# Attention with one shared key and value head, plus a gated MLP: a fifth of the exps on VectorE, all engine orders from one planner, layer norm streamed into the first group

## The chip, the cores and the metric

One core of one Trainium2 chip. The metric is the device time in microseconds (us) of one execution, the median of several runs; lower is better. Besides the time, each run gives the span of the core in the profile and the mean TensorE clock that was granted in it, as a share of full speed.

Engine names as in the profile: PE is the TensorE matmul, PEld its weight load, DVE is VectorE, ACT is ScalarE, POOL is GpSimd, SP is the DMA-issuing SyncEngine.

## The reference

```python
B, S, D, H, F = 1, 2048, 512, 32, 1792        # head size 16, all bf16
def reference(A_x, A_wq, A_wk, A_wv, A_wo, B_x, B_w1, B_w2):
    xn = layernorm(A_x)                        # eps 1e-5
    q = (xn @ A_wq) -> [1, 32, 2048, 16]       # 32 query heads
    k = xn @ A_wk ; v = xn @ A_wv              # one key and one value head, 16 wide
    p = softmax(q k^T * 16**-0.5)
    s = concat_heads(p v) @ A_wo
    g = silu(silu(xn @ B_w1) @ B_w2)
    return A_x + s * g
```

The softmax has 32 x 2048 x 2048 = 134 million exps. Held with keys on partitions, that is 1.05 million columns of 128, or 2048 *score tiles* of 128 keys x 512 queries. This sets the scale of everything below.

## The kernel before

The scores are taken in units of four and of two tiles, alternately, each unit in its own set of PSUM banks. ScalarE turns a unit into bf16 probabilities with one exp, and PE multiplies them with the values. Everything else (projections, MLP, output) is cut into small *jobs* between the units. A column of ones next to the values gives the softmax denominator. PSUM is the memory that PE writes its results into, used here as eight banks of 512 columns. Below, the score matmuls of one unit are a *score phase*; when they write into banks that ScalarE has just read, they are a *refill*; and matmuls with the values that go side by side into one bank are a *value round*. The silu of the MLP is computed by way of a tanh on ScalarE.

```python
NFILL = 1; NFILL_START = 3; NFILL_TAIL = 2          # dummy matmuls per unit
...
# units of 4 and 2 score tiles: banks 0..3 and 4..5
n = 4 if par == 0 else 2
...
# PE: the scores of a unit, then matmuls with a zero tile (they add nothing)
def emit_S(u, nfill=0):
    if u >= 2:
        pe.wait_ge(act_sem.sem, u - 1)              # ScalarE has read this set of banks
    for k, (c, g, kt, i) in enumerate(units[u]):    # four row tiles of 32 partitions
        h = pe.matmul(bank(b0 + k), lhsT=kT_sb[32*i:32*i+KP, kt*P:(kt+1)*P],
                      rhs=qT_sb[32*i:32*i+KP, c % 2, g, :], ..., tile_position=(32*i, 0))
        if last:
            for fi in range(nfill):
                h = pe.matmul(bank(b0 + k), lhsT=zero_sb[:, :], rhs=xnT_sb[:, 0, 0:NQ],
                              start=False, stop=(fi == nfill - 1))
    h.then_inc(s_sem.sem, 1)
...
# ScalarE
a.activation(p_sb[:, u % NPB, 0:n*NQ], ps[:, b0*512:(b0+n)*512], ACT.Exp)
...
# layer norm in two halves of 1024 rows: bn_stats on VectorE, Sqrt on ScalarE
# (a second activation table), transposes, K, V, Q; the first exp comes after both halves
```

The softmax here doesn't subtract the row's maximum and nothing guards it: scores larger than these inputs give would overflow.

## Time and profile before

1020.22 us, median of 3 runs (1019.31 to 1020.82).

The first lines are the page's busy times and shares of the span, then the granted clock in 40 slices (in tenths of full speed).

```profile
span 1014.8 us, 12867 instructions
...
PE 811.4 (80%) x5406; PEld 220.8 (22%) x5406; DVE 197.7 (19%) x346; ACT 977.1 (96%) x786; POOL 10.4 (1%) x13
...
PEclk8999999999999999999999999999999999999998
```

ScalarE is busy 96% of the time and VectorE 19%.

The groups of instructions, shapes kept apart (busy us, mean ns of one, idle time before them and what ended it):

```profile
L565 ACT ACTIVATE p_sb<-ps 128x2048 bf16<-128x2048 f32 x341 | 686.9, 2014 | 9.0 <-PE ps L674 3.5 <-PE ps L668 0.5
L565 ACT ACTIVATE p_sb<-ps 128x1024 bf16<-128x1024 f32 x342 | 398.9, 1166 | 1.2 <-PE ps L668 0.6 <-PE ps L674 0.5
L674 PE MATMUL ps<-xnT_sb,zero_sb 128*128 128x512 bf16 x458 | 158.8, 387 | 0.0
```

The two exp groups add up to more than ScalarE's busy time, because one ACTIVATE starts before the recorded end of the one before it. "Busy" and "idle" therefore hide small gaps. What an exp really costs is read from the distance between the start times of neighbours. Its smallest value is 1.756 us after a 2048-column exp, 0.903 after a 1024-column one and 0.476 after a 512-column tanh. From 512 to 1024 to 2048 columns it grows by 0.427 us for each 512, so I estimate from these three that a column costs 0.833 ns and a start about 50 ns. What a step takes beyond that minimum I call a **gap**. All gaps below are computed in this way from the start times of exps and tanhs.

The timeline of ScalarE at the start (start, length, both in us):

```profile
0.73 1.28 ACT L498 ACT_TABLE_LOAD   x1 [0.73 <-PEq L819]
...
20.41 0.20 ACT L498 ACTIVATE rstd_sb<-rstd_sb 128x8 f32<-128x8 f32 x1
...
24.03 1.28 ACT L522 ACT_TABLE_LOAD   x1
...
35.18 1.88 ACT L565 ACTIVATE p_sb<-ps 128x2048 bf16<-128x2048 f32 x1 [0.48 <-PE ps L674]
```

With these readings the span before is: 35.2 us until the first exp, 942.3 us of ScalarE work (341 x 1.757 + 342 x 0.903 + 72 x 0.477), 26.4 us of gaps, and 10.8 us after the last exp. Together 1014.7 of 1014.8.

### The profile page before, as it was taken

The numbers are of one execution on the slowest core, as the hardware profiler recorded it, in microseconds if no ns is written. First come the engines' busy times: TensorE is split into PE (matmuls) and PEld (weight loads), VectorE is DVE, ScalarE is ACT, GpSimd is POOL, SyncE is SP. The second block draws the span as 40 slices with busy tenths as digits, with TensorE's granted clock in tenths as the row PEclk, the third lists the DMA queues.
The fourth block names the chain that finished last, engine by engine and source line by source line (L and its number), as shares of the span: only waits on it lengthen the run. The fifth ranks groups of instructions, "written<-read, shape, count | busy, mean of one in ns | idle before, by whom it ended". The sixth has DMA issues, their size and how long they took to land.

```text
span 1014.8 us, 12867 instructions
## 1 busy us (share of the span) xinstructions
PE 811.4 (80%) x5406; PEld 220.8 (22%) x5406; DVE 197.7 (19%) x346; ACT 977.1 (96%) x786; POOL 10.4 (1%) x13
## 2 busy tenths in 40 slices
PE   3887778877788888777888887778878888888885
PEld 2322222222222222222222222222222222222221
DVE  6122122222111222212112211222102111100113
ACT  5799999999999999999999999999999999999995
POOL 4000000000000000000000000000000000000000
PEclk8999999999999999999999999999999999999998
DMA  9000000000000000000000000000000000000000
GB/s 270 1 1 1 1 1 1 1 1 1 1 1 1 12 11 1 1 1 1 1 1 11 11 1 1 1 1 2 1 1 11 11 1 1 1 1 1 2 1 21
DMA packets 7369, 9.76 MB, mean 10 GB/s; under 512 B 1488, under 2 KB 6608, under 8 KB 7312
## 3 DMA queue, kind: packets, MB, share of 16 engines
q1 hardware_dynamic: 6576, 5.28, 1.9%
q0 software_dynamic: 736, 3.67, 1.0%
q8 instruction: 42, 0.69, 0.3%
q14 instruction: 15, 0.12, 0.0%
HBM read 6.85 MB, written 2.10 MB: 9 GB/s over the span
## 4 chain that ended last, share of the span: by engine, by line
ACT 49%; PE 32%; issue 15%; DVE 3%; DMA 0%; ACTq 0%; DVEq 0%
ACT p_sb L565 45%; PE ps L668 11%; PE ps L696 9%; PE ps L674 6%; ACT t_sb L555 3%; PE ps L736 2%; PE ps L729 1%; PE ps L742 1%; DVE oraw_sb L399 1%; PE ps L771 1%; PE ps L762 1%; PE ps L594 1%; DVE stats_sb L359 0%; DMA x_sb<-in_A_x_dram 0%; ACT xnT_sb L521 0%
## 5 line engine op out<-in xcount | busy, mean ns | idle before, releaser
L565 ACT ACTIVATE p_sb<-ps 128x1024 bf16<-128x1024 f32 (+1 forms) x683 | 949.4, 1590 | 10.2 <-PE ps L674 4.0
L668 PE MATMUL ps<-qT_sb,kT_sb 32*128 32x512 bf16 x2048 | 267.5, 385 | 164.5 <-ACT p_sb L565 163.2
L696 PE MATMUL ps<-p_sb,vaug_sb 128*32 128x512 bf16 x2048 | 274.4, 390 | 9.2 <-DVE oraw_sb L399 8.5
L674 PE MATMUL ps<-xnT_sb,zero_sb 128*128 128x512 bf16 x458 | 158.8, 387 | 0.0
L668 PEld LDWEIGHTS ps<-qT_sb,kT_sb 32*128 32x128 bf16 x2048 | 66.7, 91 | 412.9 <-ACT p_sb L565 390.6
L696 PEld LDWEIGHTS ps<-p_sb,vaug_sb 128*32 128x32 bf16 x2048 | 68.9, 93 | 187.7 <-issue 152.0
L434 DVE SCALAR_TENSOR_TENSOR u_sb<-t_sb,ps 128x512 bf16<-128x512 bf16 x56 | 38.5, 687 | 263.7 <-ACT t_sb L555 263.7
L736 PE MATMUL ps<-w_sb,u_sb 128*128 128x512 bf16 x224 | 67.8, 385 | 0.7 <-DVE tmp_sb L438 0.7
L729 PE MATMUL ps<-xnT_sb,w_sb 128*128 128x512 bf16 x224 | 67.8, 385 | 0.0
L399 DVE CAST oraw_sb<-ps 128x512 bf16<-128x512 f32 x32 | 22.1, 692 | 203.8 <-PE ps L696 203.8
L555 ACT ACTIVATE t_sb<-ps 128x512 bf16<-128x512 f32 x72 | 60.0, 833 | 0.0
L674 PEld LDWEIGHTS ps<-xnT_sb,zero_sb 128*128 128x128 bf16 x458 | 35.4, 96 | 78.7 <-issue 78.0
L445 DVE TENSOR_SCALAR qT_sb<-ps 128x512 bf16<-128x512 f32 x30 | 20.6, 685 | 109.1 <-PE ps L742 109.1
L438 DVE SCALAR_TENSOR_TENSOR tmp_sb<-t_sb,ps 128x512 bf16<-128x512 bf16 x16 | 11.0, 686 | 138.5 <-ACT t_sb L555 138.5
L742 PE MATMUL ps<-xnT_sb,wqp_sb 128*128 128x512 bf16 x120 | 36.3, 385 | 0.0
L771 PE MATMUL ps<-wop_sb,xn_sb 128*128 128x512 bf16 x96 | 29.1, 385 | 0.0
L401 DVE STREAM_TRANSPOSE otr_sb<-oraw_sb 128x512 bf16<-128x512 bf16 x32 | 22.8, 712 | 1.1
L414 DVE STREAM_TRANSPOSE xn_sb<-otr_sb 128x512 bf16<-128x512 bf16 x32 | 22.8, 711 | 1.1
L418 DVE SCALAR_TENSOR_TENSOR fin_sb<-ps,tmp_sb 128x512 bf16<-128x512 f32 x12 | 8.3, 692 | 63.7 <-PE ps L771 63.7
L736 PEld LDWEIGHTS ps<-w_sb,u_sb 128*128 128x128 bf16 x224 | 12.7, 97 | 26.2 <-issue 25.2
L729 PEld LDWEIGHTS ps<-xnT_sb,w_sb 128*128 128x128 bf16 x224 | 12.8, 97 | 25.4 <-issue 25.4
L582 PE MATMUL ps<-ident,xn_sb 128*128 128x128 bf16 x64 | 5.1, 256 | 12.4 <-DVE xn_sb L376 12.4
(53 smaller groups left out, 125.8 us busy)
## 6 DMA issues: line engine op xcount, KB each, us to landing
w_sb<-in_B_w_dram POOLq DMA_DIRECT2D x2, 1792.0 KB, 13.1
x_sb<-in_A_x_dram SPq DMA_DIRECT2D x4, 512.0 KB, 5.8
out_dram<-ob_sb SPq DMA_DIRECT2D x16, 128.0 KB, 1.7
wqn_sb<-in_A_wq_dram SPq DMA_DIRECT2D x1, 512.0 KB, 7.9
wop_sb<-in_A_wo_dram SPq DMA_DIRECT2D x4, 128.0 KB, 6.6
wkn_sb<-in_A_wk_dram SPq DMA_DIRECT2D x1, 16.0 KB, 6.9
wv_sb<-in_A_wv_dram SPq DMA_DIRECT2D x1, 16.0 KB, 6.7
```

Of the source, the lines that this page charges most:

```text
L399: v.tensor_copy(oraw_sb[:, sl, :], bank(OB)).then_inc(o_sem.sem, 1)
L401: v.transpose(otr_sb[:, sl, :], oraw_sb[:, sl, :]).then_inc(dv.sem, 1)
L434: v.scalar_tensor_tensor(out=u_sb[:, tc % 2, ft, :], in0=t_sb[:, ti % 2, :], scalar=1.0, in1=bank(FB), op0=ALU.add, op1=ALU.mult).then_inc ...
L555: a.activation(t_sb[:, ti % 2, :], bank(FB), ACT.Tanh, scale=scale).then_inc(t_sem.sem, 1)
L565: a.activation(p_sb[:, u % NPB, 0:n * NQ], ps[:, b0 * 512:(b0 + n) * 512], ACT.Exp).then_inc(act_sem.sem, 1)
L668: h = pe.matmul(bank(b0 + k), lhsT=kT_sb[32 * i:32 * i + KP, kt * P:(kt + 1) * P], rhs=qT_sb[32 * i:32 * i + KP, c % 2, g, :], start=True, ...
L674: h = pe.matmul(bank(b0 + k), lhsT=zero_sb[:, :], rhs=xnT_sb[:, 0, 0:NQ], start=False, stop=(fi == nfill - 1))
L696: h = pe.matmul(bank(OB)[32 * i:32 * (i + 1), :], lhsT=vaug_sb[:, kt, :], rhs=p_sb[:, u % NPB, k * NQ:(k + 1) * NQ], start=(kt == 0), stop ...
L729: h = pe.matmul(bank(FB), lhsT=w1_sb[:, dc, ft * P:(ft + 1) * P], rhs=xnT_sb[:, dc, tc * NQ:(tc + 1) * NQ], start=(dc == 0), stop=(dc == N ...
L736: h = pe.matmul(bank(FB), lhsT=u_sb[:, tc % 2, ft, (tt % 4) * P:(tt % 4 + 1) * P], rhs=w2_sb[:, ft, :], start=(ft == 0), stop=(ft == NFT - 1))
L742: h = pe.matmul(bank(FB), lhsT=wqp_sb[:, dc, g, :], rhs=xnT_sb[:, dc, c * NQ:(c + 1) * NQ], start=(dc == 0), stop=(dc == NDC - 1))
L771: h = pe.matmul(bank(FB), lhsT=on_sb[:, (c % 2) * NG + g, (tt % 4) * P:(tt % 4 + 1) * P], rhs=wop_sb[:, g, :], start=(g == 0), stop=(g == ...
```

## The change

The intent is to take exps off the busiest engine and give them to an idle one, VectorE, without using an exp there. For a bf16 number, adding a constant to the 16-bit pattern of 2^y moves y. So VectorE computes `round(128*log2(e)*x + const)` as a 16-bit integer from the scores (the *conversion*); read as bf16 this is e^x with a straight line between powers of two. Five more integers, made by adding 21, 43, 64, 85 and 107 (the *shifts*), give the same line at other places within the octave. A weighted sum of the six is close to e^x. The weights are put into six copies of the value tile, so PE forms the sum while it multiplies with the values, at the price of six value matmuls per tile instead of one.

At the same time the whole kernel is rewritten. Every operation is a task with an estimated duration; one planner walks all engines through time and fixes each engine's order and semaphores at build time. Units become three and two tiles. The projections run as four column tiles of 32, the same array mode as the value matmuls. The dummy matmuls go. Layer norm runs in four chunks of 512 rows with `pow` on GpSimd instead of `Sqrt` on ScalarE, and the first group of heads starts when the first chunk is ready.

```diff
-NFILL = 1
-NFILL_START = 3
-NFILL_TAIL = 2
+SHIFT = (0, 21, 43, 64, 85, 107)
+SHIFT_W = (0.23925781, 0.21875, 0.19824219, 0.16210938, 0.15820312, 0.13769531)
+SHIFT_BETA = -0.603400124
+MM = 216.0
+SWITCH = 105.0
+DVE_LIMIT = 2500.0
+S_TOL = 30.0
...
+class Planner:            # clk, order and tasks per engine; place(), finalize(), run_engine()
...
+    A_BANKS = ((0, 1, 2), (3, 4))          # units of three and two tiles
...
+        for j in range(K + 1):             # K = 6
+            pl.add(Task(DV, 260.0, lambda v, j=j: v.memset(v_sb[:, j, :, :], 1.0 if j == 0 else SHIFT_W[j - 1]),
+                        (), [("V", j, c) for c in range(NC)], 0))
...
+            t2 = pl.add(Task(PO, 400.0, lambda g, a=a, b=b: g.tensor_tensor(
+                rstd_sb[:, a:b], rstd_sb[:, a:b], half_sb[:, 0:4], ALU.pow), ...
...
+                    bt.P[i] = pl.add(Task(DV, 620.0, lambda v, b=b, i=i, bb=bt.b: v.tensor_scalar(
+                        db_sb[:, bb, i * NQ:(i + 1) * NQ], bank(b), 128.0 * LOG2E, 128.0 * SHIFT_BETA + 16256.0,
+                        op0=ALU.mult, op1=ALU.add), ...                     # the conversion, 16-bit integer out
...
+                    pl.add(Task(DV, 600.0, lambda v, s=s, j=j, bb=bt.b: v.tensor_scalar(
+                        ds_sb[:, s, :], db_sb[:, bb, :], SHIFT[j], None, op0=ALU.add), ...   # a shift, 4 tiles at once
...
+        def do_S(t): ...                   # scores of a unit, and of 0 to 2 tiles for VectorE
+        def do_pv(t, got): ...             # a value round: up to four column tiles into one bank
...
+            if ts is not None:             # a score refill is coming up: hold PE back for it
+                if ts <= t + 30: ...
+                elif col is not None:
+                    if max(ts, end) > max(ts, act_need() - 446.0) + S_TOL:
+                        pl.clk[PE] = ts
+                        return True
```

The emitted program has 334 exps of 1536 columns, 333 of 1024, 72 tanh, 380 conversions, 475 shifts and 3948 value matmuls.

## The prediction

> **What bounds the kernel now.** ScalarE. The page's busy table has ACT at 977.1 of 1014.8 us (96%), PE 811 (80%, with 158.8 us of dummy matmuls against a zero tile), DVE 197.7 (19%). From the start times of neighbouring ACTIVATEs in the trace, a 2048-column exp holds ScalarE 1.756 us at least, a 1024-column one 0.903, a tanh 0.476: 0.833 ns per column plus 50 ns each. 341 x 1.756 + 342 x 0.903 + 72 x 0.476 = 942 us. The first exp starts at 35.2 us, the last work of ScalarE ends at 1004, then an 11 us tail. So 967 us of exp phase hold 942 of work and about 25 of hand-over gaps: the 1024-column exp is followed after 0.913 us at the median but 1.13 at the 95th percentile, because PE refills four banks late.
>
> **What changes.**
> 1. 380 of 2048 score tiles (19%) leave ScalarE, counted in the emitted program. It keeps 334 exps of 1536 columns (1.33 us) and 333 of 1024 (0.903), plus 72 tanh: 444 + 301 + 34 = 779 us, a saving of 163.
> 2. VectorE gains 380 affine conversions from PSUM (0.62 us spacing) = 236 us, and 475 shifts over 2048 16-bit columns in SBUF. The trace has none. [...] With old duties (tanh products 44, norm 49, prologue 25, rest 26) about 665 us.
> 3. PE drops the dummies; each moved tile needs six value matmuls instead of one. 3948 value matmuls in 1179 rounds of up to four column tiles, 667 score phases, 592 projection rounds, at 216 ns each, plus 1314 tiling switches at about 100 ns (neighbouring starts of 310 to 321 instead of 216 ns): about 660 us.
> 4. Prologue: streaming the norm by four tiles, pow on GpSimd instead of Sqrt plus a second table load. First exp near 17 us instead of 35; some starvation follows while VectorE (6 us per chunk of keys) feeds a ScalarE that needs 7 us per chunk.
>
> **How much is on the path.** All ScalarE time was, so nearly all 163 us come off, and about 18 us at the start. Engine sums are 779 / 665 / 660, so ScalarE should still bound, but three engines at 80 to 95% in one fixed order have less slack: refilling three banks must fit in a 0.903 us exp, as tightly as before, and value rounds now also wait for VectorE. I allow 40 us of gaps instead of 25. 17 + 779 + 40 + 10 = 846 in the profile; plus the 5 us by which the timed run exceeds the span: **850 us**, 8 in 10 between 825 and 890. Faster by over 2%: 0.96; within 2%: 0.02; slower: 0.02.
>
> **What would show it.** ACT busy near 810 to 830 us and still above 93%; 667 exps; [...] DVE near 80%; PE busy near 80%; first exp at 15 to 20 us; start-to-start of exps near 1.33 and 0.90 us, with PE as the main releaser of ScalarE's gaps.
>
> **What would make it wrong.** [...] consecutive rounds on the same column tiles that cost more than 216 ns [...]; a static order drifting from the plan, so that PE stalls for VectorE and starves ScalarE (900 us or more).

The 665 us of VectorE, and with it "DVE near 80%", contain the 475 shifts: the terms left, 236 for the conversions and 144 for the old duties, come to 380. That ScalarE and not VectorE would bound rested on the 665. The 7 us per chunk of keys are an estimate from the trace, 16 score tiles of 0.427 us and their starts; for VectorE's 6 us, spacings in the same trace give 4 x (0.593 + 0.065 + 0.323) us for the norm of four row tiles and 2 x 0.597 + 0.62 us for copies from PSUM, 5.7 us.

## More of the kernel before

The clock is full all through the exps (a granted share of 1.00 from 25.3 to 1008.4 us).

## The result, and the profile after

834.15 us, median of 4 runs (830.19 to 836.27), against 1019.77 us of the kernel before. The ratio is 0.817, 95% interval 0.815 to 0.820.

The page after, the same lines:

```profile
span 831.3 us, 19227 instructions
...
PE 723.5 (87%) x8492; PEld 211.9 (25%) x8492; DVE 681.4 (82%) x1159; ACT 794.5 (96%) x743; POOL 17.2 (2%) x47
...
PEclk9999999999999999999999999999999999999988
```

The groups, shapes kept apart:

```profile
L1130 ACT ACTIVATE pa_sb<-ps 128x1536 bf16<-128x1536 f32 x334 | 563.7, 1688 | 7.8 <-PE ps L677 7.3 <-PE ps L928 0.3
L1130 ACT ACTIVATE pa_sb<-ps 128x1024 bf16<-128x1024 f32 x333 | 420.3, 1262 | 2.8 <-PE ps L928 1.5 <-PE ps L677 1.3
L871 DVE TENSOR_SCALAR ds_sb<-db_sb 128x2048 uint16<-128x2048 uint16 x475 | 307.1, 683 | 2.7
L839 DVE TENSOR_SCALAR db_sb<-ps 128x512 uint16<-128x512 f32 x380 | 257.1, 684 | 93.3 <-PE ps L677 92.3
```

VectorE went from 19% to 82%, and ScalarE is still the busiest at 96%. The shifts take 683 ns each as recorded, and 0.602 us from start to start at the median. Conversions waited 92 us for scores, so VectorE was not short of time.

ScalarE's timeline at the start:

```profile
2.35 1.28 ACT L336 ACT_TABLE_LOAD   x1 [2.35 <-issue]
...
14.68 1.02 ACT L414 ACTIVATE xnT_sb<-ps 128x1024 bf16<-128x1024 bf16 x1 [10.83 <-PE ps L405]
17.70 0.60 ACT L433 ACTIVATE kt_sb<-ps 128x512 bf16<-128x512 f32 x1 [2.00 <-PE ps L390]
20.82 2.37 ACT L1130 ACTIVATE pa_sb<-ps 128x1536 bf16<-128x1536 f32 x2 [2.52 <-PE ps L677]
```

There is one table load instead of two, and the first exp is at 20.8 us instead of 35.2. The sum of the span, with the predicted terms beside it:

| us | before | predicted | after |
|---|---|---|---|
| until the first exp | 35.2 | 17 | 20.8 |
| ScalarE work (exps and tanhs) | 942.3 | 779 | 779.3 |
| gaps between them | 26.4 | 40 | 20.0 |
| after the last exp | 10.8 | 10 | 11.0 |
| span | 1014.8 | 846 | 831.3 |

Of 183.5 us gained in the span, 163.0 are ScalarE work, 14.4 are the earlier start and 6.4 are smaller gaps. The steps between exps are 1.331 us (median) after 1536 columns and 0.905 after 1024, within a few ns of the minimum.

The trace also records when the clock was halved. Before, that never happened during the exps. After, it happened seven times, for 25.9 us in all (stretches of 3.413 or 6.827 us at a share of 0.50, the last one counted up to the start of the last exp), and 8.5 of the 20.0 us of gaps end within such a window or in the microsecond after it. This is one of them on the timeline, with the clock at half until 506.1 us:

```profile
505.52 0.11 PEld L677 LDWEIGHTS ps<-qt_sb,kt_sb 32*128 32x128 bf16 x4 [0.84 <-ACT pa_sb L1130]
505.52 0.61 PE L677 MATMUL ps<-qt_sb,kt_sb 32*128 32x512 bf16 x4
506.06 0.34 PEld L390 LDWEIGHTS ps<-xnT_sb,w_sb 128*32 128x32 bf16 x12 [0.44 <-issue]
506.06 0.83 PE L390 MATMUL ps<-xnT_sb,w_sb 128*32 128x512 bf16 x12
506.19 1.45 ACT L1130 ACTIVATE pa_sb<-ps 128x1536 bf16<-128x1536 f32 x1 [0.92 <-PE ps L677]
```

The four score matmuls take 0.61 us, where 202 other phases of four take 0.39 to 0.40 at full clock, and ScalarE waits 0.92 us for them.

### The profile page after: what moved, and what is told of

Read it like the earlier page. It is cut to its first block, busy times and chain, and to the rows that moved or that the text cites. A ratio compares the mean times of both kernels' runs of the same rounds, so it can differ in the third digit from the quotient of the medians.

```text
span 831.3 us, 19227 instructions
## 1 busy us (share of the span) xinstructions
PE 723.5 (87%) x8492; PEld 211.9 (25%) x8492; DVE 681.4 (82%) x1159; ACT 794.5 (96%) x743; POOL 17.2 (2%) x47
## 4 chain that ended last, share of the span: by engine, by line
ACT 86%; PE 8%; DVE 4%; POOL 1%; issue 1%; ACTq 0%; DVEq 0%
ACT pa_sb L1130 82%; ACT t_sb L505 3%; PE ps L390 3%; PE ps L928 2%; PE ps L677 2%; DVE ds_sb L871 1%; ACT t_sb L528 1%; DVE db_sb L839 1%; DVE v_sb L334 1%; DVE stats_sb L348 1%; DVE xn_sb L367 0%; PE ps L405 0%; POOL v_sb L462 0%; POOL rstd_sb L363 0%; DVE qt_sb L485 0%
## 5 line engine op out<-in xcount | busy, mean ns | idle before, releaser
L1130 ACT ACTIVATE pa_sb<-ps 128x1536 bf16<-128x1536 f32 (+1 forms) x667 | 782.6, 1475 | 10.6 <-PE ps L677 8.6
L677 PE MATMUL ps<-qt_sb,kt_sb 32*128 32x512 bf16 x2048 | 265.4, 390 | 79.0 <-ACT pa_sb L1130 72.8
L839 DVE TENSOR_SCALAR db_sb<-ps 128x512 uint16<-128x512 f32 x380 | 257.1, 684 | 93.3 <-PE ps L677 92.3
L871 DVE TENSOR_SCALAR ds_sb<-db_sb 128x2048 uint16<-128x2048 uint16 x475 | 307.1, 683 | 2.7
L928 PE MATMUL ps<-pa_sb,v_sb 128*32 128x512 bf16 x1668 | 256.2, 390 | 1.6 <-DVE f_sb L945 1.0
L928 PE MATMUL ps<-ds_sb,v_sb 128*32 128x512 bf16 x1900 | 229.3, 389 | 3.9 <-DVE ds_sb L871 2.3
L677 PEld LDWEIGHTS ps<-qt_sb,kt_sb 32*128 32x128 bf16 x2048 | 65.6, 91 | 345.3 <-ACT pa_sb L1130 318.9
L928 PE MATMUL ps<-db_sb,v_sb 128*32 128x512 bf16 x380 | 124.3, 390 | 2.7 <-DVE f_sb L945 2.3
L390 PE MATMUL ps<-w_sb,u_sb 128*32 128x512 bf16 x896 | 73.8, 384 | 0.1
L390 PE MATMUL ps<-xnT_sb,w_sb 128*32 128x512 bf16 x896 | 72.2, 388 | 0.5 <-DVE u_sb L507 0.5
L390 PEld LDWEIGHTS ps<-xnT_sb,w_sb 128*32 128x32 bf16 x896 | 19.0, 95 | 29.8 <-issue 20.2
```

The source lines that it names most:

```text
L390: last = h.matmul(bank(b)[32 * j:32 * (j + 1), :], lhsT=lhs(j), rhs=rhs, start=start, stop=stop, tile_position=(0, 32 * j), skip_group_che ...
L677: return pe.matmul(bank(b), lhsT=kt_sb[32 * i:32 * i + 32, g % 2, kt * P:(kt + 1) * P], rhs=qt_sb[32 * i:32 * i + 32, (g // 2) % NQR, :], ...
L839: bt.P[i] = pl.add(Task(DV, 620.0, lambda v, b=b, i=i, bb=bt.b: v.tensor_scalar(db_sb[:, bb, i * NQ:(i + 1) * NQ], bank(b), 128.0 * LOG2E, ...
L871: pl.add(Task(DV, 600.0, lambda v, s=s, j=j, bb=bt.b: v.tensor_scalar(ds_sb[:, s, :], db_sb[:, bb, :], SHIFT[j], None, op0=ALU.add), [("Db ...
L928: h = pe.matmul(bank(OB)[32 * i:32 * (i + 1), :], lhsT=lhs, rhs=rhs, start=s0, stop=s1, tile_position=(0, 32 * i), skip_group_check=True)
L1130: op = pl.place(AC, 0.8333 * NQ * n + 65.0, lambda a: a.activation(pa_sb[:, s, 0:n * NQ], ps[:, b0 * 512:(b0 + n) * 512], ACT.Exp), [("ps" ...
```

## The experiments

Two theories stood against each other. **A:** ScalarE bounds both kernels, and the gain is the work that left it. **B:** most of the gain comes from the rest of the rewrite (the planned order, no dummy matmuls, the streamed norm), or PE and VectorE bound the new kernel too. The offload without the rest of the rewrite was not run. Each run was correct. Each was timed on one chip beside the kernel before; times are medians of four runs, six in the last experiment. Where I compare two variants I use their ratios to the kernel before, times 1020 us, because the four batches ran at different times.

### No tile on VectorE

```diff
         def want_d(banks_left=True):
-            if st["assigned"] < 8 or not pool_free:
-                return False
+            return False
```

> The changed kernel with its planner, streamed norm and column-tiled projections, but no score tile on VectorE: 410 exps of 1536 columns, 409 of 1024, 72 tanh, which at 1.330, 0.903 and 0.477 us is 949 us of ScalarE work against 779. If the move of the exps is the cause and ScalarE the bound: 834 + 170 = about 1000 us, so nearly all of the gain is gone. Rival, that most of the gain comes from the planned order, the dropped dummy matmuls and the streamed norm: well under 950 us.

Measured: 1051.6 us, ratio 1.030 (1.025 to 1.034). So without the offload, the rest of the rewrite is 3% slower than the kernel before, and the whole gain hangs on the offload. B's first half falls. But the loss is 217 us and not the 170 that A's sum allows. The page:

```profile
PE 903.6 (86%) x6592; PEld 217.2 (21%) x6592; DVE 161.4 (15%) x304; ACT 977.3 (93%) x895; POOL 17.1 (2%) x47
...
PEclk9978786766788878655787887666667887766656
```

The granted clock fell to 0.74. During the exps it was halved for 535 us. The work is 949.0 us as counted, the first exp is at 20.8 as in the full change, but the gaps are 69.1 us, of which 65.8 are in or just after half-speed windows; only 3.3 us are at full clock. So 170 us of work and 49 us of added gaps make up the loss (219 us in the profiled spans). The offload does something that I had not listed: with it the clock is at 0.98 and without it at 0.74, so it keeps the clock up, as the dummy matmuls had done before. That its six value matmuls per tile are what does it is not shown by this run; a count at the end of "Why the prediction was right or wrong" supports it.

### Half of the offload

```diff
             free = [k for k in range(NDB) if db_busy[k] == 0]
-            if not free:
+            if not free or 4 * st.get("nbatch", 0) > 0.095 * st["assigned"]:
                 return None
+            st["nbatch"] = st.get("nbatch", 0) + 1
```

> Half of the offload: 192 tiles on VectorE instead of 380, 863 us of ScalarE work. If ScalarE bounds all the way: 834 + 84 = about 918 us, on the straight line between none and all. Rival, that VectorE or PE already bound the full offload in part: the second half of the offload brings clearly less than the first, so this run lies well under 918.

Measured: 953.2 us, ratio 0.934. Both theories missed. The time lies above the line of A (918), where B wanted it below. Clock 0.87, gaps 52.9 us, of which 46.8 are in or just after half-speed windows and 6.1 at full clock. The work is 863 us, as planned. The first half of the offload brought 97 us and the second 119: with the second half the clock also rises, from 0.87 to 0.98.

### The kernel before without its dummy matmuls

```diff
-NFILL = 1
-NFILL_START = 3
-NFILL_TAIL = 2
+NFILL = 0
+NFILL_START = 0
+NFILL_TAIL = 0
```

> The kernel before without its 458 dummy matmuls. If they only kept the TensorE clock up: the granted clock shows windows at half speed in the middle of the run, where ScalarE then waits, and the time goes up by 5 to 40 us over 1020. Rival, that the 159 us of dummies held PE late for the refill of the score banks: the gaps of 26 us shrink and the time falls by 5 to 15 us, which would make dropping them a part of the gain.

Measured: 1030.5 us, ratio 1.008 (1.004 to 1.013). The mean clock fell to 0.813 to 0.824 over its four runs; the seven runs of the kernel before beside them had 0.974 to 0.993. The clock in 40 slices:

```profile
PEclk8888688968789999889988989878987888555567
```

Half speed for 341 us of the exp phase; gaps 36.3 us instead of 26.4, of which 31.3 in or just after half-speed windows. So the dummies kept the clock up, and taking them out alone costs 10 us (4 to 13 by the interval; within 2%). Only 5.0 us of gaps remained at full clock, though, against 26.4 before, in two thirds of the time: the dummies also seem to have made PE late for refills. Both of the expected mechanisms fit, and the clock weighs more.

### No offload, with every second score phase issued twice

```diff
-            def emit(pe, mm=tuple(mm)):
+            def emit(pe, mm=tuple(mm), more=len(units) % 2 == 1):
                 h = None
-                for (b, g, i, kt) in mm:
-                    h = s_mm(pe, b, g, i, kt)
+                for rep in range(2 if more else 1):
+                    for (b, g, i, kt) in mm:
+                        h = s_mm(pe, b, g, i, kt)
```

(On top of the edit of the first experiment.)

> No score tile on VectorE, as in the run without offload, but every second score phase (the one of two banks) issued twice, 409 x 0.216 = 88 us of matmuls that change nothing. The run without offload took 1052 us, 535 us of its exp phase at half clock, 66 of its 69 us of gaps there. If the clock is what it lost beyond ScalarE's 170 us: under 100 us at half speed, and 995 to 1015 us. Rival, that the planned order without the offload has gaps for other reasons: over 1035 us.

This failed as an instrument. Measured: 1149.6 us, ratio 1.126, and the clock went down, to 0.71:

```profile
PE 1046.8 (91%) x7410; PEld 227.2 (20%) x7410; DVE 161.2 (14%) x304; ACT 1009.9 (88%) x895; POOL 17.1 (1%) x47
...
PEclk9988865766766796676586867655675687666656
```

Half speed for 660 us, gaps 168.9 us, of which 163.2 in or just after half-speed windows, 5.7 at full clock. The PE row is busy 91% of the span and the clock is granted least of all. So "PE busy" doesn't tell whether the clock is kept. What the repeated two-tile score phases lack, against the dummies of the kernel before (whole 128 x 128 tiles) or the value rounds, was not separated; the count at the end of "Why the prediction was right or wrong" bears on it. The run does repeat the reading of the first experiment: at full clock (here about four tenths of the exp phase) the planned order has gaps of 3 to 6 us, and the rest comes with the half-speed windows. What the rewrite would take without offload at full clock was therefore not measured.

### 34 us more on ScalarE

```diff
+        def twice(a, out_, in_, scale):
+            a.activation(xtra_sb[:], in_, ACT.Tanh, scale=scale)
+            return a.activation(out_, in_, ACT.Tanh, scale=scale)
...
-            t1 = Task(AC, 492.0, lambda a: a.activation(t_sb[:, k, :], bank(b), ACT.Tanh, scale=0.5), ...
+            t1 = Task(AC, 492.0, lambda a: twice(a, t_sb[:, k, :], bank(b), 0.5), ...
```

(The other tanh, with scale 0.25, likewise. The plan isn't told.)

> The changed kernel with every tanh computed a second time into scratch, outside the plan: 72 x 0.477 = 34 us more on ScalarE alone. If ScalarE bounds: 834 + 34 = 868 us, at least 28 of the 34 visible. Rival, that PE or VectorE set the pace: under 10 us visible.

Measured: 873.2 us, ratio 0.856, so 40 us more. All 34 us are seen. The added 6 lie in the gaps, 26.1 us in all: those in or just after half-speed windows rose from 8.5 to 16.9 us (57 us at half speed instead of 26), and those at full clock fell from 11.5 to 9.1. ScalarE bounds, one for one.

### 35 us more on VectorE

```diff
-                    pl.add(Task(DV, 600.0, lambda v, s=s, j=j, bb=bt.b: v.tensor_scalar(...
+                    def shift(v, s=s, j=j, bb=bt.b, more=st["nsh"] % 8 == 0):
+                        if more:
+                            v.tensor_scalar(xtra_sb[:], db_sb[:, bb, :], SHIFT[j], None, op0=ALU.add)
+                        return v.tensor_scalar(ds_sb[:, s, :], db_sb[:, bb, :], SHIFT[j], None, op0=ALU.add)
+                    pl.add(Task(DV, 600.0, shift, ...
```

> One shift in eight done a second time into scratch, outside the plan: 59 x 0.60 = 35 us more on VectorE alone (681 to 716 busy of 831). If VectorE has slack: under 10 us more than 834. Rival, that VectorE is a joint bound or that the fixed order has no slack for delays: 25 to 35 us more.

Measured: 841.8 us, ratio 0.826, so 8 to 9 of the 35 us are seen. Gaps at full clock rose from 11.5 to 20.1 us. VectorE has slack for three quarters of the delay. The last quarter shows the price of a fixed order: a delay that the plan did not know of reaches ScalarE by way of PE. In the trace, weight loads for value rounds wait 77.9 us for shifts instead of 40.1, and the exps wait 13.1 us for PE instead of 10.4 (as recorded, so without the small gaps).

### 36 us more on PE, before two-bank and before three-bank refills

The same doubled score phases as above with the offload in place: every fourth unit, once at `len(units) % 4 == 3` (a two-bank unit), once at `% 4 == 2` (a three-bank unit). The tiles whose scores go to VectorE in that phase are doubled with it.

> Every fourth score phase issued twice (same result), outside the plan: 167 x 0.216 = 36 us more on PE alone. The doubled phase delays the refill of a score bank that ScalarE waits for, and the hand-over had no slack in front of three-bank refills: I expect about half of them to be seen, 10 to 25 us more. If PE had slack everywhere: under 5. If PE were the bound: 36.

Measured: 830.7 us, ratio 0.814 (0.811 to 0.818). None of the 36 us is seen. My expectation was wrong, and in part for a careless reason: the doubled units are two-bank ones, refilled during a 1.33 us exp, not the tight three-bank ones. The clock rose a little, from 0.973 to 0.985 over the four runs of the change to 0.987 to 0.991. So I doubled the other kind:

> As the run with doubled score phases that cost nothing (36 us of PE work, all in two-bank phases), but the doubled ones are three-bank phases, one in two: 167 x 0.216 = 36 us again. A three-bank refill has to fit in the 0.903 us of a 1024-column exp, where the hand-over just fits; a two-bank refill has 1.33 us. If PE's slack lies before the two-bank refills alone: most of the 36 us are seen, 850 to 868 us. Rival, that PE has slack everywhere: within 5 us of 831.

Measured: 832.7 us, ratio 0.816 (0.812 to 0.820); the expectation of 850 or more fell. Gaps at full clock rose from 11.5 to 15.5 us, those around half-speed windows fell from 8.5 to 4.7. In front of the doubled refills the median step after a 1024-column exp is 0.954 us; in front of the others it is 0.903. So some 50 ns of the 216 are seen and the rest is hidden: PE has room before both kinds of refill, about 0.17 us before the tight one.

### Without the rule that holds PE back before a refill

```diff
-S_TOL = 30.0
+S_TOL = 1e9
```

> The planner no longer holds PE back before a score refill that is about to fall due (392 tiles move, 6 us less ScalarE work). If this rule is why the gaps were 20 us and not the 40 that I allowed: three-bank refills come up to 0.3 us late, the median step from a 1024-column exp to the next rises from 0.905 to 1.0 or more, and the time rises by 20 to 80 us. Rival, that the gaps are small because PE has room anyway: within 8 us of 834.

Measured: 843.8 us (836.2 to 846.2), ratio 0.826: 8 us more, although this plan moved 392 tiles and so left ScalarE 5.3 us less work. The profiled run, the fastest of the four at 836.2, had 29.0 us of gaps, 20.0 at full clock. Both sides of the expectation missed: it is less than 20 us more, and just over the 8 of the rival. The median step after a 1024-column exp stayed at 0.904 us, against what I expected; the upper quartile grew, from 0.921 to 1.029. The rule is worth some 9 us of gaps in the profiled runs and about 13 us by the times (8 + 5), so about half of the distance between the 20 us of gaps and the 40 that I had allowed. The room that PE has before refills (the experiment before) is a likely part of the rest.

### Scores only when all keys are there

```diff
-            if g >= NG:
+            if g >= NG or any(c not in evac_kt or evac_kt[c].op is None for c in range(NC)):
                 return None
```

> The first score phase waits until all 2048 keys are normalised and projected, so nothing is streamed into the first group (392 tiles move instead of 380, 6 us less ScalarE work). If streaming is worth the time by which exps start earlier: the first exp moves from 20.8 us to about 40 to 45 us and the time rises by about that less 6, to 848 to 855 us. Rival, that the early exps run so starved that streaming brings little: within 5 us of 834.

Measured: 842.7 us, ratio 0.826, 8 us more, with 5.3 us less ScalarE work. The first exp moved from 20.8 to 38.9 us:

```profile
17.70 0.60 ACT L433 ACTIVATE kt_sb<-ps 128x512 bf16<-128x512 f32 x1 [2.00 <-PE ps L390]
38.90 3.71 ACT L1130 ACTIVATE pa_sb<-ps 128x1536 bf16<-128x1536 f32 x3 [20.60 <-PE ps L677]
```

Of 18.1 us of later start, 3.5 come back as smaller gaps and 5.3 as less work. At 8 us the cost is below the 14 to 21 that I expected and above the rival's 5. With the lighter work added back, streaming is worth about 14 us.

### Filling up value rounds with zero tiles

```diff
+            have = {m[0]: m for m in mm}
+            some = next(iter(have.values()))[2]
+            mm = [have.get(i, (i, zero_sb[:], some, False, False)) for i in range(4)
+                  if i in have or 0 < done[g, i] < tot[g, i]]
```

(And a zero tile, set by GpSimd.)

> Value rounds that fill fewer than four column tiles are filled up with matmuls of a zero stationary tile (714 more)[...]. If the half-speed windows of the clock (26 us of the exp phase in the changed kernel, with 8.5 of its 20 us of gaps in or just after them) come from too little work in the array, and zero tiles count as work: fewer than 10 us at half speed and 5 to 8 us less, about 828. Rival, that zero or partly filled tiles do not count: clock and time as without.

Measured: 832.8 us (827.9 to 833.3), ratio 0.815 (0.811 to 0.820), against 0.817 (0.815 to 0.820) of the change. The profiled run was the fastest, with 12.6 us at half speed and a clock of 0.989; the three others had 0.981, a value that the change has too. Inconclusive.

### The memsets of the value tiles moved

```diff
-            pl.add(Task(DV, 260.0, lambda v, j=j: v.memset(v_sb[:, j, :, :], 1.0 if j == 0 else SHIFT_W[j - 1]),
-                        (), [("V", j, c) for c in range(NC)], 0))
+            pl.add(Task(PO, 700.0, lambda g, j=j: g.memset(v_sb[:, j, :, :], 1.0 if j == 0 else SHIFT_W[j - 1]),
+                        (), [("V", j, c) for c in range(NC)], 0 if j == 0 else 2))
```

(With the doubled two-bank score phases, which cost nothing.)

> The seven memsets of the value tiles (5.5 us on VectorE ahead of the layer norm, which starts at 7.8 us although its input should land near 4) go to GpSimd, six of them at a lower priority; the doubled score phases that cost nothing and went with a clock of 0.99 (830.7 us) stay in. If those memsets are why the first exp came at 20.8 us and not at the 17 that I predicted: the norm starts at 4 to 5 us, the first exp at 17 to 18.5, and the time is 826 to 829 us. Rival, that the start is held by loads, by GpSimd's pow or by PE: the first exp stays within 1 us of 20.5 and the time at 831.

VectorE's timeline of the change first, then of this run:

```profile
2.33 5.54 DVE L334 MEMSET v_sb<- 128x768 bf16 x7
7.79 2.41 DVE L348 BATCH_NORM_STATS2 stats_sb<-ds_sb 128x6 f32<-128x512 bf16 x4
10.11 0.36 DVE L351 BATCH_NORM_AGGREGATE mv_sb<-stats_sb 128x2 f32<-128x6 f32 x4
11.96 1.38 DVE L367 TENSOR_SCALAR xn_sb<-ds_sb,mv_sb,rstd_sb 128x512 bf16<-128x512 bf16 x4 [1.49 <-POOL rstd_sb L363]
```

```profile
3.72 2.47 DVE L348 BATCH_NORM_STATS2 stats_sb<-ds_sb 128x6 f32<-128x512 bf16 x4 [1.50 <-DMA ds_sb<-in_A_x_dram]
6.11 0.36 DVE L351 BATCH_NORM_AGGREGATE mv_sb<-stats_sb 128x2 f32<-128x6 f32 x4
8.95 1.38 DVE L367 TENSOR_SCALAR xn_sb<-ds_sb,mv_sb,rstd_sb 128x512 bf16<-128x512 bf16 x4 [2.48 <-POOL rstd_sb L363]
```

The norm starts when its load lands, at 3.72 us instead of 7.79, and the first exp is at 17.8 instead of 20.5 (the same kernel without the moved memsets). Measured: 829.0 us (826.0 to 829.9), ratio 0.811 (0.809 to 0.814): 3.3 us less than with the doubled phases alone, and the lowest median. The intervals of the two ratios overlap (0.809 to 0.814 and 0.811 to 0.818) and the two profiled spans differ by only 1.0 us, since the gaps are 20.2 us instead of 18.2; so the earlier first exp is shown, and the gain in time is not clear of noise. One microsecond of the four is lost again: VectorE now waits 2.48 us for GpSimd's `pow` instead of 1.49, because GpSimd is still busy with a memset, which ends at 7.49 us, a microsecond after the statistics are ready at 6.47.

## Why the prediction was right or wrong

The time, 834 us, lies within 825 to 890 and 16 us under the 850 predicted. The mechanism was right; three terms of the sum were mis-sized. In the profiled run the start was 3.8 us longer than predicted, the gaps 20.0 shorter, the tail 1.0 longer and the time above the span 3.2 shorter, so the errors partly cancelled; the 40 us of gaps were an allowance and not worked out.

- **The bound and the work.** Right. ScalarE work 779.3 us for 779 predicted, 34 us added to ScalarE appear in full, 35 us added to VectorE by a quarter, 36 us added to PE not at all. The page has ACT at 794.5 us, 96% ("near 810 to 830" was too high). VectorE at 82% and PE at 87% are near the 80% that I gave for both.
- **The shifts.** Measured: on 2048 columns of 16-bit integers 683 ns as recorded and 0.602 us from start to start at the median, so 475 of them make 286 us. With the 380 us of the other terms that is 666 us of VectorE work, and the page has it busy for 681.4.
- **The start.** "First exp near 17 us": 20.8. The step that failed is the list of what VectorE does before the norm. Seven memsets of 768 columns take 5.54 us, 0.81 each from start to start, where the planner puts 0.26. Memsets of 256, 768 and 1024 elements (32-bit, bf16 and 32-bit) are recorded at 272, 698 and 912 ns in this trace, 0.83 ns more per element. I took the plan's 0.26 as it stood. Moving them brought the first exp to 17.8 us.
- **The gaps.** "I allow 40 us": 20.0. I took PE to have no slack before a three-bank refill. It has about 0.17 us (most of a doubled phase is hidden), and the planner's rule keeps refills on time (9 us of gaps without it). "PE as the main releaser" of the gaps holds.
- **The timed run above the span.** I added 5 us, the difference between two different runs of the kernel before. In the runs that have both it is 1.8 us, at most 2.4.
- **The dummies.** "PE drops the dummies" stood in the prediction as a pure saving on PE. That the dummies held the clock, and that the offload holds it in their place, was missing. It did not hurt the sum, because both kernels have a nearly full clock. It would have hurt any prediction of a part: the rewrite without offload is 51 us slower than its ScalarE sum says (1052 against about 1000).

What stays open: why the clock is still halved for some 26 us in the change, and which property of the matmuls keeps it up. Repeated score phases went with a slightly higher clock with the offload (0.987 to 0.991) and a lower one without it (0.71).

A count from the traces narrows this down. The clock changes on a grid of 3.413 us (in the trace of the change every full-speed or half-speed stretch but the last, which the span cuts off, is a multiple of that). For each stretch of this grid I take the matmuls that start in it, give each one of 512 columns 0.216 us (their spacing at full clock) times the share that its weight tile has of a 128 x 128 tile, the largest in the traces, and divide the sum by 3.413 us. This *array share* is an estimate. In all 14 traces together, from 60 us to 40 us before the end, none of 2286 full-speed stretches with a share of 0.4 or more was followed by a half-speed one; from 0.3 to 0.4 it was 48 of 320, and below 0.3 it was 147 of 179. The means by run:

| run | PE busy | array share | granted clock |
|---|---|---|---|
| change | 87% | 0.57 | 0.98 |
| before | 80% | 0.48 | 0.99 |
| half of the offload | 84% | 0.44 | 0.87 |
| before, no dummies | 79% | 0.38 | 0.82 |
| no offload, phases doubled | 91% | 0.35 | 0.71 |
| no offload | 86% | 0.34 | 0.74 |

The four halvings of the change within these limits came after shares of 0.30 to 0.40. By this count a two-tile score phase (two weight tiles of 32 x 128 side by side) has half of a 128 x 128 tile, a value round of four (128 x 32 each) all of it, which fits the run that failed as an instrument. The limit is not sharp (the kernel before had 42 stretches below 0.4 and no halving), and no run set the array share alone: this is an order in time, not a tested cause.

## What to carry to other kernels

Find what the busiest engine really costs per instruction from start-to-start distances, count its instructions in the emitted program, and the sum predicts the time to a few per cent, as long as small delays added to the other engines stay hidden. Work moved to an idle engine can pay even at six times the matmuls, if PE has room for them. Before dropping dummy matmuls or thinning PE's work, look at the granted clock: PE can be busy 86% and still run at three quarters of its clock; the estimated array share (0.34 in that run, 0.48 in the kernel before) told more here than how long it was busy.

## What else the traces show

- Short idle times of PE do not mean that the clock is kept. In the run without offload, the longest idle time of PE during the exps is 1.1 us, and the clock is halved for 535 us of that phase; in the kernel before without dummies 1.9 us and 341 us; in the kernel before itself it is 1.2 us, and the clock is full.
- PE at 91% busy, with repeated score phases in row tiles of 32, had a mean clock of 0.71; the kernel before, at 80% with dummies of 128 x 128, had 0.99. Weighted by the array share, the matmuls separate the stretches that are followed by half speed: 147 of 179 below 0.3, none of 2286 from 0.4 up.
- In the change, rounds of four column tiles of 128 rows follow one another at 0.216 to 0.227 us from start to start (lower quartile, three quarters). The loads of 32 columns are recorded under the matmuls: from 302.11 us of the span, the 12 loads of three rounds take 0.34 us, and their 12 matmuls 0.83 us from the same start.
- Back to back, the 2048-column shift on 16-bit integers takes 0.602 us from start to start, not the 0.683 of its record.
- The recorded times of memsets of three sizes (272, 698 and 912 ns for 256, 768 and 1024 elements) grow by 0.83 ns per element.
- `pow` on GpSimd, four elements per partition, takes 1.04 us as recorded, on the way to the first exp.
